# A linear-attention and Fourier-mixing kernel: the last additions and stores move into the other way of the closing branch, and the middle row's products get a stationary operand of 128 columns

## The chip, the cores and the metric

The kernel runs on one core of one Trainium2 chip. TensorE (PE) multiplies matrices, with the weight loads in a queue of their own (PEld); VectorE (DVE), ScalarE (ACT) and GpSimd (POOL) work element by element; SyncE (SP) issues transfers. A "q" behind an engine's name in a row of the profile stands for its sequencer: loads of registers, branches, waits and issues of transfers. The metric is the time of one execution on the device in microseconds (us), as the median of several runs; lower is better.

## The reference

The inputs are q, k, v and a gate, each of 4 batches, 8 heads, 768 steps and 48 channels, and two weight matrices of 384x1536 and 1536x384. All is float32 in the kernel.

```python
f = 1.0 / (1.0 + np.exp(-f_logit))
for t in range(S):
    state = f[:, :, t, :, None] * state + np.einsum('bhd,bhe->bhde', k[:, :, t], v[:, :, t])
    y[:, :, t] = np.einsum('bhd,bhde->bhe', q[:, :, t], state)
...
x = np.ascontiguousarray(attn_out.transpose(0, 2, 1, 3)).reshape(B, S, H * D)
...
X = np.fft.fft(x, axis=1)
X = np.fft.fft(X, axis=2)
mixed = np.real(X).astype(np.float32)
u = x + mixed
mu = np.mean(u, axis=-1, keepdims=True)
var = np.mean((u - mu) ** 2, axis=-1, keepdims=True)
un = (u - mu) / np.sqrt(var + 1e-06)
ch = np.maximum(un @ w_ch1, 0.0) @ w_ch2
return (u + ch).astype(np.float32)
```

## The kernel before

The kernel has four stages for each of the 4 batches, and works on several batches at once.

*Attention* works on 16 units (two heads of a batch each), in blocks of 128 steps: `attention`, `outputs`, `fold`. It leaves x, of 6 blocks of 128 tokens by 384 channels, and sums and differences of x for the Fourier stage in the tiles `ce`, `se`, `xc`, `xs`.

*The Fourier stage* is `fnet`: products with cosine and sine tables over the tokens (tile `z`, L740), over the channels (tile `mix`, L759, two blocks of tokens by symmetry), and for the middle row of the batch, a single token that belongs to no block, two products into the tile `mid` (L774). Their stationary operand is one column of `zz`, so they use one column of TensorE's array and write one row. In the program's terms a float32 product becomes two weight loads and two multiplications in the trace; the 8 products of the four batches are 16 rows. In batch 3 `mid` and `mix` stand in the middle of the previous batch's first layer (L861); in the others they stand behind products of the attention, of 48 rows and 64 columns.

*Normalisation* is `turn`: mean, deviation, and a turned copy of each block.

*The two layers* are `projected`, for a pair of blocks c and d at a time. The first layer (`hidden`, L861) forms 15 products by a scheme that saves some of 18, and the second one (L916) forms 7 products of 6 multiplications each where 8 would stand, from h and from sums of the second weight matrix made ahead. A pair's results are the halves c1, c2 of block c and d1, d2 of block d. They are gathered in two banks: tile `fx` has the halves X and Y, tile `fz` the halves V and Z. Product 6 goes on top of product 1 in X, product 7 on top of both; products 5 and 3 go into Z. The last pair of the last batch is (0, 4), and has an order of its own (L937 to L954): c1 is stored as soon as it is whole (L938), then come products 6, 5, 7 and 3. VectorE adds V to d1 (L940), X after product 6 to c2 (L943), Z after product 5 to d2 (L946), X after product 7 to d1 and d2 in one instruction (L949), which makes block d (token block 4) whole. SyncE stores it in three pieces (L714). Product 3 goes on top of product 5 in Z, and c2 gets Z with both in one addition (L952) and is stored last (L953).

*The order of all this* is written out by hand: the string `ORDER` holds 964 words, and each word takes one step of a stage (`P3` is one step of the last batch's `projected`). A step ends at a `yield`. Each engine runs its own instructions in that order.

*The general way.* The fast program is right for inputs within some bounds. The step `judge` (L984 to L994) works out a flag from what the kernel saw; it stands some 35 us ahead of the end. Behind the last step each engine loads the flag into a register (L1045) and branches on it (L1047). With the flag set, a general program of about 8000 instructions runs, which computes all again; with it not set, as with these inputs, the engines jump over it. In the code there is no other way, only the compiler's own: it waits until the engine's work is done, and sets the semaphores as the general program would have left them. Behind both stand the closing waits (L1131): SyncE waits for every transfer and every engine, and then the five engines meet twice.

SyncE's load of the flag is followed by two register instructions that check its bounds (FUSED_REGOPS and SEQ_ASSERT in the trace).

Of the kernel before, what the change touches and what calls it, by code (L numbers as in the profile page):

```python
# [7 lines left out]
F32 = mybir.dt.float32  # L8
U32 = mybir.dt.uint32
AF = mybir.ActivationFunctionType  # L10
ALU = mybir.AluOpType

C = 128
# [77 lines left out]
def kernel(  # L91
# [40 lines left out]
    y_out = ps_y.tile([128, 2, 512], F32, tag="y", name="y")  # L132
    spare = y_out[:, 0, 3 * C:]

    def fixed(shape, tag):
        return const.tile(shape, F32, tag=tag, name=tag)

# [3 lines left out]
    g_t = [fixed([128, S + 1], f"g{i}") for i in range(2)] + [wide_t[:, i * (S + 1):(i + 1) * (S + 1)] for i in range(2)]  # L141
    k_t = [fixed([128, S], f"k{i}") for i in range(2)] + [wide_t[:, 2 * S + 2:3 * S + 2]]
    q_t = [fixed([128, S], f"q{i}") for i in range(2)] + [wide_t[:, i * S + 2:(i + 1) * S + 2] for i in range(3, 5)]
    few = [True]

    def home(name, u):

        if few[0] and u >= 2 * HP:
# [569 lines left out]
    def fnet(b, x):  # L718
# [12 lines left out]
        rows_of = [hi - lo for _, lo, hi in terms]  # L731
        for T in (1, 3, 0, 2):
            src, lo, hi = terms[T]
            z = ps_f.tile([128, 512], F32, tag="f", name=f"z{b}_{T}")[:hi - lo]
            if T % 2 == 0:
                parts = [(slice(0, N), 3, 1), (slice(0, NQ, 2), 1, 0), (slice(1, NQ, 2), 0, 0), (OD, 2, 0)]
            else:
                parts = [(slice(0, N), 0, 1), (EV, 1, 0), (OD, 2, 0)]
            for i, (cols, j, t) in enumerate(parts):
                nc.tensor.matmul(z[:, cols], lhsT=src[:, j, lo:hi], rhs=tab[:, t, T % 2, cols],  # L740
                                 start=(i == 0), stop=(i == len(parts) - 1), skip_group_check=True)
            falls = down(z)[:, :QS // 2 - 1:-1]
            nc.scalar.copy(pairs(zz[:hi - lo, T, :QS]), up(z)[:, :QS // 2])
            nc.scalar.copy(pairs(zz[:hi - lo, T, 2 * C:3 * C]), falls[:, :C // 2])
            nc.scalar.copy(pairs(zz[:hi - lo, T, QS:2 * C]), falls[:, C // 2:])
            if T % 2 == 0:
                nc.scalar.copy(zz[:hi - lo, T, 3 * C:3 * C + 1], z[:, QS // 2:QS // 2 + 1])
            yield
# [2 lines left out]
        mv = p2.tile([128, NCH, 2], F32, tag="mv", name=f"mv{b}")  # L751
        rstd = p2.tile([128, NCH], F32, tag="rstd", name=f"rstd{b}")
        def mixed(c):
            mix = ps_f.tile([128, 512], F32, tag="f", name=f"mix{b}_{c}")
            for odd in range(2):
                o = slice(0, NQ) if not odd else slice(NQ, N)
                for i in range(2):
                    T = 2 * odd + i
                    nc.tensor.matmul(mix[:, o], lhsT=zz[:rows_of[T], T, PLACES[c]],  # L759
                                     rhs=cd[:rows_of[T], T, :NQ - odd], start=(i == 0), stop=(i == 1))  # L760
            return mix
# [3 lines left out]
        falling = lambda a, n: a[:, 1:2 * n - 1].rearrange("p (r m) -> p m r", r=2)[:, ::-1]  # L765


        mid = ps_f.tile([128, 512], F32, tag="f", name=f"mid{b}")
        row = p1.tile([128, DM], F32, tag="row", name=f"row{b}")
        by2 = lambda a: a.rearrange("p (m r) -> p m r", r=2)  # L770
        H1 = QD + 1
        for T, o in ((0, slice(0, H1)), (2, slice(H1, 2 * H1 - 1))):
            n = rows_of[T]
            nc.tensor.matmul(mid[0:1, o], lhsT=zz[:n, T, 3 * C:3 * C + 1], rhs=cd[:n, T, :o.stop - o.start],  # L774
                             start=True, stop=True)
        nc.vector.tensor_tensor(by2(row[0:1, :HD]), rising(mid[0:1], H1), by2(x[0:1, 3, :HD]), ALU.add)
        nc.vector.tensor_tensor(by2(row[0:1, HD:]), falling(mid[0:1], H1), by2(x[0:1, 3, HD:]), ALU.add)
# [12 lines left out]
        def turn(c):  # L790
            j, t = [(j, pair.index(c)) for j, pair in enumerate(pairs_of) if c in pair][0]
            if t == 0:
                turned[j] = p2.tile([128, 3, 2, 128], F32, tag="unT", name=f"unT{b}_{j}")
            un = p2.tile([128, DM], F32, tag="un", name=f"un{b}_{c}")
            nc.vector.tensor_scalar(un, x[:, c], mv[:, c, 0:1], rstd[:, c:c + 1], ALU.subtract, ALU.mult)
            yield
            pt = ps_f.tile([128, 512], F32, tag="f", name=f"pt{b}_{c}")
            for kt in range(3):
                nc.tensor.transpose(pt[:, kt * 128:(kt + 1) * 128], un[:, kt * 128:(kt + 1) * 128], ident)  # L799
            nc.scalar.copy(turned[j][:, :, t], pt[:, :DM].rearrange("p (k t) -> p k t", k=3))  # L800
# [42 lines left out]
    def hidden(name, unT, h):  # L843

        tokens = lambda i: unT[:, i % 3, i // 3 ^ FLIP] if i < 6 else sums[:, i - 6]
        opened = set()
        chains = {i: ps_a.tile([128, 512], F32, tag="sc", name=f"{name}_{i}") for i in range(2)}  # L850
        for made, a, w, chain, to, how, complete in PRODUCTS:
            for i, one, two, sign in made:
                add(tokens(i), tokens(one), tokens(two), sign)
            if made:
                yield
            new = chain not in opened
            opened.add(chain)
            if chain not in chains:
                chains[chain] = ps_f.tile([128, 512], F32, tag="f", name=f"{name}_{chain}")
            for m in range(4):  # L860
                nc.tensor.matmul(chains[chain][:, m * 128:(m + 1) * 128], lhsT=block(w)[:, m * 128:(m + 1) * 128],  # L861
                                 rhs=tokens(a), start=(new and m == 0), stop=True, skip_group_check=True)
            out = h[:, to % 3 * 4:to % 3 * 4 + 4, to // 3 ^ FLIP]
            got = chains[chain].rearrange("p (m n) -> p m n", n=128)
            first = how[0] == "="
            if first:
                kind = AF.Relu if complete else AF.Copy
                nc.scalar.activation(out, got, kind, scale=1.0 if how == "=+" else -1.0)  # L868
            else:
                nc.vector.tensor_tensor(out, out, got, ALU.add if how == "+" else ALU.subtract)  # L870
            if complete and not first:
                yield
                nc.scalar.activation(out, out, AF.Relu)  # L873
            yield

    def projected(b, x, again=False):
# [5 lines left out]
        for j, (c, d) in enumerate(PAIRS if b < B - 1 else LAST_PAIRS):  # L882
# [5 lines left out]
            if b and not again:  # L888
                yield from hidden(f"ub{b}_{j}", turned_of[b][j], h)
            for m in range(NF if again or not b else 0):  # L890
                pp = ps_f.tile([128, 512], F32, tag="f", name=f"up{b}_{j}_{m}")
                for kt in range(3):
                    nc.tensor.matmul(pp[:, :256], lhsT=w1[:, kt, m * 128:(m + 1) * 128], rhs=unT[:, kt],  # L893
                                     start=(kt == 0), stop=(kt == 2))
                nc.scalar.activation(h[:, m].rearrange("p t n -> p (t n)"), pp[:, :256], AF.Relu)  # L895
                yield
            if not again and (b, j) == (0, 0):

                for t, i in enumerate((c, d)):
                    po = ps_f.tile([128, 512], F32, tag="f", name=f"po{b}_{i}")  # L900
                    for m in range(NF):
                        nc.tensor.matmul(po[:, :DM], lhsT=h[:, m, t], rhs=w2[:, m],  # L902
                                         start=(m == 0), stop=(m == NF - 1))
                        if m in (2, 5, 8):
                            yield
                    tt(x[:, i], po[:, :DM], x[:, i], ALU.add)
                    store(b, i, x[:, i])
                    yield
                continue
# [6 lines left out]
                    nc.tensor.matmul(out, lhsT=h[:, m], rhs=blocks[i][:, m], start=(start and m == 0),  # L916
                                     stop=(m == H - 1), skip_group_check=True)

            fx = ps_f.tile([128, 512], F32, tag="f", name=f"fx{b}_{j}")
            X, Y = fx[:, :HD], fx[:, HD:2 * HD]  # L920
            product(1, X, h11, start=True)
            s1 = p1.tile([128, H, 128], F32, tag="s1", name=f"s1_{b}_{j}")
# [4 lines left out]
            tt(c1, X, c1, ALU.add)  # L927
            tt(h11, s1, h11, ALU.subtract)
            yield
            fz = ps_f.tile([128, 512], F32, tag="f", name=f"fz{b}_{j}")  # L930
            V, Z = fz[:, :HD], fz[:, HD:2 * HD]
            product(4, V, h22, start=True)
            tt(c1, Y, c1, ALU.add)
# [1 line left out]
            yield  # L935
            both = x[:, d].rearrange("p (a n) -> p a n", a=2)
            if (b, c) == (B - 1, 0):  # L937
                nc.sync.dma_start(out=out[b, :C, :HD], in_=c1)  # L938
                product(6, X, h11)
                tt(d1, V, d1, ALU.add)  # L940
                yield
                product(5, Z, s1)
                tt(c2, X, c2, ALU.add)  # L943
                yield
                product(7, X, h21)
                tt(d2, Z, d2, ALU.add)  # L946
                yield
                product(3, Z, h12)
                tt(both, X.unsqueeze(1).to_broadcast([128, 2, HD]), both, ALU.add)  # L949
                store(b, d, x[:, d])  # L950
                yield
                tt(c2, Z, c2, ALU.add)  # L952
                nc.sync.dma_start(out=out[b, :C, HD:], in_=c2)  # L953
                yield  # L954
                continue
            product(5, Z, s1)
# [13 lines left out]
            store(b, d, x[:, d])  # L970
            yield

    x_of, units, fronts, rest = {}, {}, {}, {}

    def x_all(b):
        if b not in x_of:
# [3 lines left out]
    def judge():  # L980
# [6 lines left out]
        nc.vector.tensor_scalar(most, most, SMALLEST, None, ALU.is_lt)  # L987
        nc.vector.scalar_tensor_tensor(most[:R], part[:R, 0:1], HIGH, most[:R], ALU.is_ge, ALU.max)
        nc.vector.scalar_tensor_tensor(most[:R], part[:R, 1:2], WARM, most[:R], ALU.is_ge, ALU.max)
        turned = ps_f.tile([128, 512], F32, tag="f", name="turned")  # L990
        nc.tensor.matmul(turned[0:1, :128], lhsT=most, rhs=ident, start=True, stop=True)
        nc.vector.tensor_reduce(most[0:1], turned[0:1, :128], mybir.AxisListType.X, ALU.max)
        flag = p1.tile([128, 1], mybir.dt.int32, tag="flag", name="flag")
# [50 lines left out]
    tc.no_sync_barrier()  # L1044
    again = nc.values_load(flag[0:1, 0:1], min_val=0, max_val=1)  # L1045
    few[0] = False
    with tc.If(again > 0):  # L1047
        if wide:
            for i, (dst, _, _) in enumerate(blocks_of):
                single_or_zero(dst, words(i))  # L1050
# [7 lines left out]
        for b in range(B):  # L1058
# [5 lines left out]
                pass  # L1064
            for _ in projected(b, x, again=True):
                pass


# [67 lines left out]
```

## Time and profile before

| what | value |
|---|---|
| median of 3 runs | 517.89 us (517.5 to 519.24) |
| the profiled execution | 521.55 us |
| its span, first to last instruction | 519.8 us |
| mean granted clock of TensorE | 0.98 |
| TensorE, multiplications | busy 488.9 us, 94% |
| TensorE, weight loads | busy 450.3 us, 87% |
| VectorE | busy 375.6 us, 72% |
| ScalarE | busy 217.6 us, 42% |
| GpSimd | busy 62.4 us, 12% |

The span lies within one profiled execution, which takes 1.75 us more than its span; the runs without a profile are shorter than the profiled one. Rows of the profile read "line engine operation out<-in". In a timeline the two first numbers are the start in us from the span's start and the length. In the rows of one line, three numbers with strokes between them are the shortest, median and longest duration in ns, and then come the first and the last start. L numbers are lines of the kernel before; the changed kernel's stand some 5 to 17 lower down.

### The profile page before, as it was taken

Reading aid. Unit: us, or ns where it says so; the run is one execution under the profiler, and the core shown is the slowest. Engines: PE = TensorE matmul, PEld = TensorE weight load, DVE = VectorE, ACT = ScalarE, POOL = GpSimd, SP = SyncE. Lnnn points to the kernel's source line nnn. Section 1 sums busy time; section 2 is a strip of 40 time slices with the busy share of each in tenths; the row PEclk is TensorE's granted clock in tenths of the full one; section 3 lists DMA queues with packets and bytes.
Section 4 is the critical chain, followed back from the end, with each engine's and each line's share of the span. In section 5 each row is a group of like instructions: output and inputs, shape, how many; then the busy total and the mean of one; then the engine's idle time right before and its main releaser. Section 6 shows DMA issues by size and latency. Waiting matters only on the chain.

```text
span 519.8 us, 13729 instructions
## 1 busy us (share of the span) xinstructions
PE 488.9 (94%) x5814; PEld 450.3 (87%) x5814; DVE 375.6 (72%) x746; ACT 217.6 (42%) x520; POOL 62.4 (12%) x85
## 2 busy tenths in 40 slices
PE   4588799989999999999999999999999999999994
PEld 4477678856898899999999899999999999999894
DVE  3868999864887478687687897689486658576561
ACT  6666469753442532462452445351431404032220
POOL 3114534541001000000001001000001000010100
PEclk9967999999999999999999999999999999999998
DMA  8987555585100420222210032101301214433001
GB/s 215 251 230 233 139 153 171 168 236 151 54 1 32 109 57 6 66 71 71 71 55 32 21 91 72 47 3 45 109 6 44 74 47 137 151 122 93 33 9 29
DMA packets 20649, 48.15 MB, mean 93 GB/s; under 512 B 3425, under 2 KB 6178, under 8 KB 20578
## 3 DMA queue, kind: packets, MB, share of 16 engines
q1 hardware_dynamic: 19474, 43.63, 29.7%
q0 software_dynamic: 1104, 3.54, 1.9%
q8 instruction: 48, 0.79, 0.7%
q14 instruction: 23, 0.19, 0.1%
HBM read 42.44 MB, written 4.72 MB: 91 GB/s over the span
## 4 chain that ended last, share of the span: by engine, by line
PE 82%; DMA 7%; DVE 3%; issue 2%; POOL 2%; ACT 2%; SPq 1%; DVEq 0%; POOLq 0%; ACTq 0%
PE ub L861 23%; PE fx L916 17%; PE fz L916 13%; PE up L893 8%; PE z L740 4%; DMA raw<-in_w_ch_dram 4%; PE mix L759 3%; PE y L568 3%; PE y L627 2%; PE po L902 2%; DMA k<-in_qkf_dram 2%; PE sc L409 2%; PE ds L610 2%; PE pt L799 1%; DMA tab<-in_seq_tab_dram 1%
## 5 line engine op out<-in xcount | busy, mean ns | idle before, releaser
L870 DVE TENSOR_TENSOR h<-h,ub 128x512 f32<-128x512 f32 x81 | 55.3, 685 | 36.7 <-PE ub L861 29.0
L708 POOL DMA_INDIRECT out_dram<-x,place x16 | 17.0, 1065 | 353.1 <-DVE x L966 227.6
L868 ACT ACTIVATE h<-ub 128x512 f32<-128x512 f32 x54 | 32.0, 593 | 46.8 <-PE ub L861 31.1
L893 PE MATMUL up<-unT,w 128*128 128x256 f32 x216 | 50.3, 383 | 0.0
L861 PE MATMUL ub<-wide,w 128*128 128x128 f32 x360 | 45.5, 276 | 2.4 <-DVE wide L833 2.4
L916 PE MATMUL fx<-block,h 128*128 128x192 f32 x264 | 46.6, 327 | 0.0
L861 PEld LDWEIGHTS ub<-wide,w 128*128 128x128 f32 x360 | 42.8, 192 | 3.4 <-PE pt L799 1.6
L916 PE MATMUL fx<-w,h 128*128 128x192 f32 x264 | 45.2, 327 | 0.0
L893 PEld LDWEIGHTS up<-unT,w 128*128 128x128 f32 x216 | 39.9, 190 | 5.7
L873 ACT ACTIVATE h<-h 128x512 f32<-128x512 f32 x45 | 28.4, 631 | 37.2 <-DVE h L870 37.2
L916 PEld LDWEIGHTS fx<-block,h 128*128 128x128 f32 x264 | 43.4, 190 | 0.1
L916 PEld LDWEIGHTS fx<-w,h 128*128 128x128 f32 x264 | 42.7, 190 | 0.2
L292 POOL TENSOR_TENSOR w<-w,raw 128x384 uint32<-128x384 uint32 x24 | 29.4, 1231 | 64.7 <-ACT raw L288 23.3
L861 PE MATMUL ub<-unT,w 128*128 128x128 f32 x288 | 36.9, 275 | 0.0
L861 PEld LDWEIGHTS ub<-unT,w 128*128 128x128 f32 x288 | 34.6, 192 | 0.0
L800 ACT COPY unT<-pt 128x384 f32<-128x384 f32 x24 | 11.3, 470 | 42.0 <-PE pt L799 41.7
L861 PE MATMUL ub<-unT,wide 128*128 128x128 f32 x216 | 28.7, 276 | 0.0
L861 PE MATMUL ub<-wide 128*128 128x128 f32 x216 | 28.5, 275 | 0.0
L386 DVE TENSOR_TENSOR_SCAN W<-g,bound 112x768 f32<-112x768 f32 x12 | 21.1, 1762 | 7.5 <-ACT g L380 7.5
L861 PEld LDWEIGHTS ub<-unT,wide 128*128 128x128 f32 x216 | 26.3, 192 | 0.2
L861 PEld LDWEIGHTS ub<-wide 128*128 128x128 f32 x216 | 26.3, 192 | 0.0
L895 ACT ACTIVATE h<-up 128x256 f32<-128x256 f32 x36 | 13.7, 382 | 25.9 <-PE up L893 25.9
(194 smaller groups left out, 996.8 us busy)
## 6 DMA issues: line engine op xcount, KB each, us to landing
raw<-in_w_ch_dram SPq DMA_DIRECT2D x24, 384.0 KB, 4.0
v<-in_v_dram SPq DMA_DIRECT2D x16, 288.0 KB, 4.8
k<-in_w_ch_dram SPq DMA_DIRECT2D x12, 384.0 KB, 3.8
g<-in_w_ch_dram SPq DMA_DIRECT2D x12, 384.0 KB, 3.2
k<-in_qkf_dram SPq DMA_DIRECT2D x14, 288.0 KB, 5.9
g<-in_qkf_dram SPq DMA_DIRECT2D x12, 288.0 KB, 5.4
q<-in_qkf_dram SPq DMA_DIRECT2D x12, 288.0 KB, 4.9
wide<-in_qkf_dram SPq DMA_DIRECT2D x10, 288.0 KB, 5.1
```

Of the source, the lines that this page charges most:

```text
L292: nc.gpsimd.tensor_tensor(bits, bits, lo, ALU.add)
L386: nc.vector.tensor_tensor_scan(W, g, bound[:R], 0.0, ALU.add, ALU.min)
L568: nc.tensor.matmul(y[FILL[g], c // 3, c % 3 * C + t.start:c % 3 * C + t.stop], lhsT=vals[rows, o:o + (64 if g == 0 else D)], rhs=weights, ...
L708: nc.gpsimd.indirect_dma_start(out=out.rearrange("b s d -> (b s) d"), out_offset=bass.IndirectOffsetOnAxis(ap=place[:, b, i:i + 1], axis=0 ...
L740: nc.tensor.matmul(z[:, cols], lhsT=src[:, j, lo:hi], rhs=tab[:, t, T % 2, cols], start=(i == 0), stop=(i == len(parts) - 1), skip_group_c ...
L759: nc.tensor.matmul(mix[:, o], lhsT=zz[:rows_of[T], T, PLACES[c]], rhs=cd[:rows_of[T], T, :NQ - odd], start=(i == 0), stop=(i == 1))
L861: nc.tensor.matmul(chains[chain][:, m * 128:(m + 1) * 128], lhsT=block(w)[:, m * 128:(m + 1) * 128], rhs=tokens(a), start=(new and m == 0) ...
L868: nc.scalar.activation(out, got, kind, scale=1.0 if how == "=+" else -1.0)
L870: nc.vector.tensor_tensor(out, out, got, ALU.add if how == "+" else ALU.subtract)
L873: nc.scalar.activation(out, out, AF.Relu)
L893: nc.tensor.matmul(pp[:, :256], lhsT=w1[:, kt, m * 128:(m + 1) * 128], rhs=unT[:, kt], start=(kt == 0), stop=(kt == 2))
L916: nc.tensor.matmul(out, lhsT=h[:, m], rhs=blocks[i][:, m], start=(start and m == 0), stop=(m == H - 1), skip_group_check=True)
```

## The change

There are three edits.

*The other way of the branch gets work.* The generator of the last pair stops behind product 3 until a list `closing` has an entry, which it gets when the branch is opened. The steps left are taken in an `Else` of the branch. They are four additions of VectorE and four stores of SyncE. The addition of Z to d2, which stood ahead of the branch, is among them. Product 3 no longer goes on top of product 5 in Z but into `last`, a piece of the bank `y_out`, which is the attention's. So c2 now gets Z (product 5) and `last` (product 3) in two additions. The results c2, d1 and d2 are gathered in the tile `xc` in place of x; ScalarE copies d2 there ahead of the branch.

*Other banks for the general way.* `bank` hands out the tiles that `fnet`, `turn`, `hidden`, `projected` and `judge` used to take from the pool `ps_f`: from that pool in the fast program, and from the attention's pool `ps_a` in the general one.

*The middle row.* The stationary operand of the two products, one column of `zz`, is read 128 times over, so that all 128 columns of the array hold the same numbers and all 128 rows of `mid` come out alike. The first row alone is used, as before.

```diff
+    def bank(name):
+        if few[0]:
+            return ps_f.tile([128, 512], F32, tag="f", name=name)
+        return ps_a.tile([128, 2, 512], F32, tag="sc", name=name)[:, 0]
...
-            nc.tensor.matmul(mid[0:1, o], lhsT=zz[:n, T, 3 * C:3 * C + 1], rhs=cd[:n, T, :o.stop - o.start],
+            nc.tensor.matmul(mid[:, o], lhsT=zz[:n, T, 3 * C:3 * C + 1].to_broadcast([n, 128]), rhs=cd[:n, T, :o.stop - o.start],
                              start=True, stop=True)
...
             if (b, c) == (B - 1, 0):
+                ends = xc.rearrange("p a n -> p (a n)")
+                c2_, d_ = ends[:, :HD], ends[:, HD:3 * HD]
+                last = y_out[:, 0, :HD]
                 nc.sync.dma_start(out=out[b, :C, :HD], in_=c1)
+                nc.scalar.copy(d_[:, HD:], d2)
                 product(6, X, h11)
-                tt(d1, V, d1, ALU.add)
+                tt(d_[:, :HD], V, d1, ALU.add)
                 yield
                 product(5, Z, s1)
-                tt(c2, X, c2, ALU.add)
+                tt(c2_, X, c2, ALU.add)
                 yield
                 product(7, X, h21)
-                tt(d2, Z, d2, ALU.add)
                 yield
-                product(3, Z, h12)
+                product(3, last, h12, start=True)
+                while not closing:
+                    yield
+                tt(d_[:, HD:], Z, d_[:, HD:], ALU.add)
+                tt(c2_, Z, c2_, ALU.add)
+                both = d_.rearrange("p (a n) -> p a n", a=2)
                 tt(both, X.unsqueeze(1).to_broadcast([128, 2, HD]), both, ALU.add)
-                store(b, d, x[:, d])
+                store(b, d, d_)
                 yield
-                tt(c2, Z, c2, ALU.add)
-                nc.sync.dma_start(out=out[b, :C, HD:], in_=c2)
+                tt(c2_, last, c2_, ALU.add)
+                nc.sync.dma_start(out=out[b, :C, HD:], in_=c2_)
                 yield
                 continue
...
-    with tc.If(again > 0):
+    with tc.If(again > 0) as both_ways:
+        closing.append(True)
...
+    with both_ways.Else():
+        for _ in rest[B - 1]:
+            pass
```

VectorE at the end of the last pair, before the change; x is the tile of the results, fx and fz the two banks, and the general way's instructions come behind the branch:

```order
L940 TENSOR_TENSOR x_3998<-fz_2_5185,x_3998 128x192
L943 TENSOR_TENSOR x_3998<-fx_2_5167,x_3998 128x192
L946 TENSOR_TENSOR x_3998<-fz_2_5185,x_3998 128x192
L949 TENSOR_TENSOR x_3998<-fx_2_5167,x_3998 128x384
L952 TENSOR_TENSOR x_3998<-fz_2_5185,x_3998 128x192
L1045 TENSOR_LOAD flag
L1047 COMPARE_AND_BRANCH
```

VectorE at the same place after the change; the rows left out are the general way, and the last four additions are the other way of the branch:

```order
L949 TENSOR_TENSOR xc<-fz_2_5185,x_3998 128x192
L952 TENSOR_TENSOR xc<-fx_2_5167,x_3998 128x192
L1058 TENSOR_LOAD flag
L1060 COMPARE_AND_BRANCH
...
L959 TENSOR_TENSOR xc<-fz_2_5185,xc 128x192
L960 TENSOR_TENSOR xc<-fz_2_5185,xc 128x192
L962 TENSOR_TENSOR xc<-fx_2_5167,xc 128x384
L965 TENSOR_TENSOR xc<-y,xc 128x192
```

The load of the flag and the branch have moved ahead of three additions, and a fourth addition, from the bank y, stands behind them.

SyncE at the end, before the change; the first row stores c1, the next three block d, the fifth c2:

```order
L938 DMA out_dram<-x_3998 128x192
L714 DMA out_dram<-x_3998 1x384
L714 DMA out_dram<-x_3998 15x384
L714 DMA out_dram<-x_3998 112x384
L953 DMA out_dram<-x_3998 128x192
L1045 TENSOR_LOAD flag
L1045 ISA x2
L1047 COMPARE_AND_BRANCH
```

SyncE at the same place after the change, again with the general way left out:

```order
L946 DMA out_dram<-x_3998 128x192
L1058 TENSOR_LOAD flag
L1060 COMPARE_AND_BRANCH
...
L719 DMA out_dram<-xc 1x384
L719 DMA out_dram<-xc 15x384
L719 DMA out_dram<-xc 112x384
L966 DMA out_dram<-xc 128x192
...
L1058 ISA x2
```

Four stores have moved behind the branch, and the two register instructions (the row with ISA) behind both ways.

More of the change, by code (lines that the diff above doesn't have):

```diff
@@ L133 @@
     spare = y_out[:, 0, 3 * C:]
+    def bank(name):
+        if few[0]:
+            return ps_f.tile([128, 512], F32, tag="f", name=name)
+        return ps_a.tile([128, 2, 512], F32, tag="sc", name=name)[:, 0]
+    few = [True]
     def fixed(shape, tag):
@@ L143 @@
     q_t = [fixed([128, S], f"q{i}") for i in range(2)] + [wide_t[:, i * S + 2:(i + 1) * S + 2] for i in range(3, 5)]
-    few = [True]
     def home(name, u):
@@ L733, in fnet @@
             src, lo, hi = terms[T]
-            z = ps_f.tile([128, 512], F32, tag="f", name=f"z{b}_{T}")[:hi - lo]
+            z = bank(f"z{b}_{T}")[:hi - lo]
             if T % 2 == 0:
@@ L753, in mixed @@
         def mixed(c):
-            mix = ps_f.tile([128, 512], F32, tag="f", name=f"mix{b}_{c}")
+            mix = bank(f"mix{b}_{c}")
             for odd in range(2):
@@ L765, in fnet @@
         falling = lambda a, n: a[:, 1:2 * n - 1].rearrange("p (r m) -> p m r", r=2)[:, ::-1]
-        mid = ps_f.tile([128, 512], F32, tag="f", name=f"mid{b}")
+        mid = bank(f"mid{b}")
         row = p1.tile([128, DM], F32, tag="row", name=f"row{b}")
@@ L796, in turn @@
             yield
-            pt = ps_f.tile([128, 512], F32, tag="f", name=f"pt{b}_{c}")
+            pt = bank(f"pt{b}_{c}")
             for kt in range(3):
@@ L858, in hidden @@
             if chain not in chains:
-                chains[chain] = ps_f.tile([128, 512], F32, tag="f", name=f"{name}_{chain}")
+                chains[chain] = bank(f"{name}_{chain}")
             for m in range(4):
@@ L890, in projected @@
             for m in range(NF if again or not b else 0):
-                pp = ps_f.tile([128, 512], F32, tag="f", name=f"up{b}_{j}_{m}")
+                pp = bank(f"up{b}_{j}_{m}")
                 for kt in range(3):
@@ L899, in projected @@
                 for t, i in enumerate((c, d)):
-                    po = ps_f.tile([128, 512], F32, tag="f", name=f"po{b}_{i}")
+                    po = bank(f"po{b}_{i}")
                     for m in range(NF):
@@ L917, in product @@
                                      stop=(m == H - 1), skip_group_check=True)
-            fx = ps_f.tile([128, 512], F32, tag="f", name=f"fx{b}_{j}")
+            fx = bank(f"fx{b}_{j}")
             X, Y = fx[:, :HD], fx[:, HD:2 * HD]
@@ L929, in projected @@
             yield
-            fz = ps_f.tile([128, 512], F32, tag="f", name=f"fz{b}_{j}")
+            fz = bank(f"fz{b}_{j}")
             V, Z = fz[:, :HD], fz[:, HD:2 * HD]
@@ L971, in projected @@
             yield
-    x_of, units, fronts, rest = {}, {}, {}, {}
+    x_of, units, fronts, rest, closing = {}, {}, {}, {}, []
     def x_all(b):
@@ L989, in judge @@
         nc.vector.scalar_tensor_tensor(most[:R], part[:R, 1:2], WARM, most[:R], ALU.is_ge, ALU.max)
-        turned = ps_f.tile([128, 512], F32, tag="f", name="turned")
+        turned = bank("turned")
         nc.tensor.matmul(turned[0:1, :128], lhsT=most, rhs=ident, start=True, stop=True)
```

## The prediction

> **What bounds the kernel now.** I read the page of the profile first, then the chain of waits over the last 40 us, then the timeline of the last 10 us, and last the single rows of the lines on which the closing branch stands, because the chain ends well before the span does. First the page:
>
> ```profile
> span 519.8 us, 13729 instructions
> ...
> PE 488.9 (94%) x5814; PEld 450.3 (87%) x5814; DVE 375.6 (72%) x746; ACT 217.6 (42%) x520; POOL 62.4 (12%) x85
> ...
> L861 PE MATMUL ub<-wide,w 128*128 128x128 f32 x360 | 45.5, 276 | 2.4 <-DVE wide L833 2.4
> ```
>
> TensorE is busy for 94% of the span, so nearly anywhere only an edit to its work can pay. The end is another matter. The chain of waits, its last pieces (start, length, what):
>
> ```profile
> 509.10 1.95 PE fx L916 x12
> 511.05 1.96 PE fz L916 x12
> ```
>
> TensorE's last product ends at 513.02 (511.05 + 1.96), and the span is 519.8. The timelines of the end (start, length) show VectorE's additions, SyncE's stores and ScalarE's last work:
>
> ```profile
> 507.19 0.36 DVE L943 TENSOR_TENSOR x<-fx,x 128x192 f32<-128x192 f32 x1 [1.28 <-PE fx L916]
> 509.14 0.36 DVE L946 TENSOR_TENSOR x<-fz,x 128x192 f32<-128x192 f32 x1 [1.59 <-PE fz L916]
> 511.09 0.56 DVE L949 TENSOR_TENSOR x<-fx,x 128x384 f32<-128x384 f32 x1 [1.59 <-PE fx L916]
> 513.04 0.36 DVE L952 TENSOR_TENSOR x<-fz,x 128x192 f32<-128x192 f32 x1 [1.39 <-PE fz L916]
> ```
>
> ```profile
> 504.84 0.34 SPq L938 DMA_DIRECT2D out_dram<-x  x1
> 511.72 1.46 SPq L714 DMA_DIRECT2D out_dram<-x  x3
> 513.42 0.35 SPq L953 DMA_DIRECT2D out_dram<-x  x1
> ```
>
> ```profile
> 499.60 0.58 ACT L868 ACTIVATE h<-ub 128x512 f32<-128x512 f32 x1
> ```
>
> VectorE's last addition ends at 513.40, so 6.4 us follow in which nothing is computed. What comes then is in the rows of the flag's load (L1045), of the branch (L1047) and of the closing lines (L1131); a row gives count, duration in ns, first and last start:
>
> ```profile
> L1045 DVEq TENSOR_LOAD <-flag x1: 541/541/541, 513.1 to 513.1; - x1
> L1045 SPq TENSOR_LOAD <-flag x1: 470/470/470, 513.8 to 513.8; - x1
> L1045 SPq FUSED_REGOPS  x1: 186/186/186, 514.4 to 514.4; - x1
> ```
>
> ```profile
> L1047 SPq EVENT_SEMAPHORE  x8: 17/17/17, 517.3 to 517.9; - x8
> ...
> L1047 ACTq COMPARE_BRANCH  x1: 50/50/50, 499.9 to 499.9; - x1
> L1047 ACTq EVENT_SEMAPHORE  x1: 17/17/17, 502.4 to 502.4; - x1
> L1047 PEldq COMPARE_BRANCH  x1: 3731/3731/3731, 510.5 to 510.5; - x1
> L1047 DVEq COMPARE_BRANCH  x1: 72/72/72, 513.7 to 513.7; - x1
> L1047 PEldq EVENT_SEMAPHORE  x1: 51/51/51, 514.3 to 514.3; - x1
> L1047 SPq COMPARE_BRANCH  x1: 50/50/50, 514.7 to 514.7; - x1
> L1047 DVEq EVENT_SEMAPHORE  x1: 21/21/21, 516.8 to 516.8; - x1
> ```
>
> ```profile
> L1131 SPq EVENT_SEMAPHORE  x14: 17/28/28, 517.9 to 519.8; - x14
> ...
> L1131 SPq DRAIN  x3: 7/13/116, 518.7 to 519.5; - x3
> ```
>
> The time from issue to landing of the last store, L953:
>
> ```profile
> DMA to landing us min/median/max: 1.8/1.8/1.8
> ```
>
> From an engine's branch to its first instruction behind it pass 2.4 us (ScalarE, 499.9 to 502.4), 2.6 (SyncE), 3.1 (VectorE) and 3.8 (TensorE), though the branch itself mostly takes 0.05 to 0.07. SyncE branches only after its last store, at 514.7, and is back at 517.3. That last store landed at 513.42 + 1.8 = 515.2, two us earlier. So the end is set by SyncE standing at its branch, with VectorE (back at 516.8) close behind; then come eight waits, the closing waits and the meetings of the engines, to 519.8. I take the standing time for the load of the code behind the branch. The Trainium skill, Runtime: NRT & Kernel Launch, section Instruction fetch mechanics, says that a taken branch to code outside the loaded pages must fetch it before going on; the rows agree, 2.4 to 3.8 us each.
>
> **The change part by part. The branch.** Behind product 6's addition (L943) VectorE now goes to the branch, and SyncE behind the store of L938. Four additions, four stores stand behind it. Each engine's stand at the branch so lies beside TensorE's products 7 and 3.
>
> VectorE: its load began with the last addition (513.04 and 513.1), the branch 0.6 later. So the branch stands at 507.2 + 0.6 = 507.8, and VectorE is back at 507.8 + 3.1 = 510.9. Until then it has nothing to miss: the product that L949 needs ends at 511.05. With 0.1 for a wait, the first addition starts at 511.0. L946's addition, moved here, and the new one that adds product 5 to c2 cost 0.36 each, as L946; L949's costs 0.56: end 511.0 + 0.36 + 0.36 + 0.56 = 512.3, where it ended at 511.65. The last addition waits for product 3 as before (513.04) and has 0.7 us of room.
>
> SyncE: it branches at 504.84 + 0.34 + 0.5 for the load, some 505.7, and is back by 508.3 (at its own 2.6) or 509.5 (at TensorE's 3.8), before VectorE's 512.3. Its three stores then start at 512.3 instead of 511.72, 0.6 later. The old last store waited for the last addition (513.40, issue 513.42); the new one waits for the three issues, 1.46 + 0.24 as before: 512.3 + 1.7 = 514.0. It lands at 514.0 + 1.8 = 515.8. SyncE itself issues until 514.35, has four waits left (eight took 0.6, so 0.3) and the two register instructions that now stand behind both ways (514.4 to 514.7, 0.3), and reaches the closing waits at 515.0. Twelve of the fourteen take 517.9 to 518.7, 0.067 each; the eighth is the last store's, reached 0.5 us after the first, 515.5, so it waits for the landing, 515.8. From the eighth wait to the end it took 519.8 - 518.4 = 1.4 (1.45 unrounded). New end 515.8 + 1.45 = 517.25: 2.55 us earlier. What is late next is no longer the branch but the landing of the last store, with the issue of three stores ahead of it.
>
> The bounds: with ScalarE's 2.4 VectorE is back at 510.2, and the additions wait for product 7 only, so stores start at 511.72 and the last at 513.42: end 516.65, gain 3.2. With TensorE's 3.8 everything is 0.7 later, gain 1.85. Inside the 1.46 one issue was slow:
>
> ```profile
> L714 SPq DMA_DIRECT2D out_dram<-x x15: 249/351/751, 120.3 to 512.4; - x15
> ```
>
> The longest issue took 0.75, the median is 0.35: three at the median give back 0.4, within these bounds.
>
> Edits with one answer: ScalarE's copy of 128x192 runs after its last work at 500.2, ten us before VectorE's use, at less than the 0.58 of that 128x512 row; its branch, 0.5 later, is hidden the same. If that cover went, it would cost its 0.58. Product 3 in a bank of its own saves TensorE nothing: the addition that it waited for ended at 509.50 and the product starts at 511.05. The scratch tile under the new results was last read by the batch's first products, which stand ahead of the middle row's at 376.45. The general way with its other banks does not run here.
>
> **The middle row.** The weight loads of the middle row and the products behind it, then the timeline of TensorE where the last of the four batches comes to it, and the first batch:
>
> ```profile
> L774 PEld LDWEIGHTS mid<-cd,zz x16: 79/83/86, 65.5 to 376.6; 97*1 97x1 f32 x8, 96*1 96x1 f32 x8
> ```
>
> ```profile
> L759 PE MATMUL mix<-cd,zz x96: 323/326/431, 65.9 to 383.4; 96*128 96x192 f32 x48, 97*128 97x193 f32 x24, 95*128 95x193 f32 x24
> ```
>
> ```profile
> 375.80 0.72 PE L861 MATMUL ub<-wide,w 128*128 128x128 f32 x5
> 376.45 0.49 PE L774 MATMUL mid<-cd,zz 97*1 97x97 f32 x4
> 376.88 1.41 PE L759 MATMUL mix<-cd,zz 97*128 97x193 f32 x7
> ```
>
> ```profile
> 65.01 0.55 PE L585 MATMUL sc<-q,g 48*64 48x64 f32 x24
> 65.49 0.49 PE L774 MATMUL mid<-cd,zz 97*1 97x97 f32 x4
> 65.91 1.09 PE L759 MATMUL mix<-cd,zz 97*128 97x193 f32 x5
> ```
>
> A 128-column stream runs at (0.72 - 0.28) / 4 = 0.11 us an instruction, five in 0.72 with 0.28 for the last. Its fifth starts at 376.25, the one-column products not at 376.36 but at 376.45, and the first product after them takes 0.43 where 0.33 is the median: going to one column and back costs 0.1 each time. Four mids at 0.11 in the stream end at 376.36 + 0.44 = 376.80, against 376.88 + 0.1 = 376.98: 0.18 us saved. In the first batch the stream ahead is of 64 columns, so one break stays: 65.49 + 0.1 + 0.44 = 66.03 against 65.91 + 0.1 = 66.01, nothing. With two further batches like the first, -0.1 in sum. The ends: -0.7 (0.18 in all four) and +0.5 (sixteen instructions 0.03 longer, 0.08 to 0.11). That a single column is read 128 times over, no row shows. The Trainium skill, TensorEngine Tiling (Array Packing), Key Properties, says that changing the tiling mode drains the array. By that rule each batch loses one break of about 0.1 and the last two, and the sum would be -0.5.
>
> Sum: -2.55 - 0.1 = -2.65 us. The profiled execution took 521.55 for its 519.8 span, 3.7 above the median of the runs, 517.89; I take the change off both: 518.9 there, span 517.15, and 515.2 for the median.
>
> **The rivals.** *A second stand.* Code of the new way that lies in two pieces stops VectorE or SyncE once more. For it: the way now holds waits, additions and stores. Against it: SyncE runs all its closing waits, 517.3 to 519.8, with no stop. VectorE back at 510.9 + 2.6 = 513.5 ends the third addition at 514.9; everything is 2.6 later, the gain is gone: 517.8. SyncE alone, stopped after its last store, has the landing as cover for 0.8 of it: its closing waits start at 515.0 + 2.6 = 517.6 and take 1.9 to the end, 519.5: gain 0.3 + 0.1, 517.5.
>
> *It does not do so much outside the profile.* The runs are 3.7 us shorter than the profiled execution; if loads of code are a part of that, SyncE's 2.6 may be 1.4 there, and the gain 1.35 + 0.1: 516.4. Against it: that difference can lie anywhere in the 520 us.
>
> *Slower: the stand moves in front of the stores.* The Trainium skill's section on instruction fetch speaks against running work behind a taken branch. In this kernel: if VectorE stands twice at the longest row, 3.8, it is back at 507.8 + 7.6 = 515.4, ends the third addition at 516.8, and the stores start at 516.8 instead of 511.72. That is 4.5 later than forecast: 4.5 - 2.65 = 1.85 slower, 519.7. It decides from a stand of 507.8 to 513.5 on, 5.7 us, nearly twice VectorE's row.
>
> **How the numbers follow.** About 0.3%, 1.55 us, is what a measurement of this kernel can tell from no change. Forecast, 515.2: chance 0.68. Its own range is 517.89 - 3.2 - 0.7 = 514.0 to 517.89 - 1.85 + 0.5 = 516.5. Second stand 0.15, less outside the profile 0.10, slower 0.07. Faster by over 0.3% (under 516.3): 0.68. Within: the two middle rivals, less than 0.01 of them beyond, 0.24. Slower: 0.08. The range 514.0 to 517.6 takes in the forecast, the third case and the half of the second, and leaves out less than 2 in 10.
>
> **What would show it.** VectorE's and SyncE's branches near 507.8 and 505.7, their first instructions behind it near 510.9 and 508.4; the last addition at 513.0 as now; the last store issued at 513.4 to 514.0; closing waits that end on its landing; a span of some 517.2. Mids at 0.11 us in the stream. It is wrong if either engine's first instruction behind the branch comes after 513, if a second gap stands behind it, or if TensorE's last product moves by more than 0.7 us.

## The result, and the profile after

The changed kernel took 514.83 us in the median of 22 runs, the kernel before 517.91 in the median of 22 beside them. The ratio is 0.9938, with a 95% interval from 0.9921 to 0.9954: 3.2 us less, between 2.4 and 4.1. The forecast was 2.65 us less. Here and below, where a ratio is given, the difference in us is worked out from it, and the ratio is not exactly that of the two medians (3.1 us here).

The profiled execution took 513.87 us, for a span of 512.1. Its page, the same rows as before:

```profile
span 512.1 us, 13731 instructions
...
PE 490.7 (96%) x5814; PEld 453.2 (88%) x5814; DVE 377.4 (74%) x747; ACT 217.5 (42%) x521; POOL 60.4 (12%) x85
```

The last pieces of its chain of waits:

```profile
500.79 1.95 PE fx L921 x12
502.74 1.95 PE fz L921 x12
504.69 1.95 PE fx L921 x12
506.64 1.96 PE y L921 x12
```

These are products 6, 5, 7 and 3. TensorE's last product ends at 508.60, and 3.5 us follow to the end of the span. Before they were 6.8 (513.02 to 519.8). I call this stretch the tail and read each kernel's from its own last product, since one execution differs from the next by more than the change. VectorE and SyncE at the end:

```profile
502.77 0.36 DVE L952 TENSOR_TENSOR xc<-fx,x 128x192 f32<-128x192 f32 x1 [1.28 <-PE fx L921]
506.40 0.36 DVE L959 TENSOR_TENSOR xc<-fz,xc 128x192 f32<-128x192 f32 x1 [3.27 <-issue]
506.67 0.35 DVE L960 TENSOR_TENSOR xc<-fz,xc 128x192 f32<-128x192 f32 x1
506.94 0.55 DVE L962 TENSOR_TENSOR xc<-fx,xc 128x384 f32<-128x384 f32 x1
508.62 0.36 DVE L965 TENSOR_TENSOR xc<-y,xc 128x192 f32<-128x192 f32 x1 [1.14 <-PE y L921]
```

```profile
500.43 0.34 SPq L946 DMA_DIRECT2D out_dram<-x  x1
507.51 1.41 SPq L719 DMA_DIRECT2D out_dram<-xc  x3
509.10 0.36 SPq L966 DMA_DIRECT2D out_dram<-xc  x1
```

The branches and the first instructions behind them are in the rows of three lines, the branch (L1060), the first addition behind it (L959) and the closing waits (L1148), whose semaphores SyncE now meets first:

```profile
L1060 SPq COMPARE_BRANCH  x1: 50/50/50, 501.4 to 501.4; - x1
L1060 DVEq COMPARE_BRANCH  x1: 72/72/72, 503.4 to 503.4; - x1
L1060 PEldq COMPARE_BRANCH  x1: 3881/3881/3881, 506.1 to 506.1; - x1
L1060 PEldq EVENT_SEMAPHORE  x1: 51/51/51, 510.1 to 510.1; - x1
```

```profile
L959 DVEq EVENT_SEMAPHORE  x1: 49/49/49, 506.3 to 506.3; - x1
```

```profile
L1148 SPq EVENT_SEMAPHORE  x18: 17/28/28, 504.0 to 512.1; - x18
```

The stands are all still there: VectorE's from 503.4 to 506.3, SyncE's from 501.4 to 504.0, 2.9 and 2.6 us. VectorE's gap is the 3.27 in the row of L959, put down to "issue", time in which it waited for nothing that the profile shows. But SyncE's lies beside products 6 and 5 and VectorE's beside 5 and 7, and both are over before product 3 begins at 506.64. TensorE's own stand, from 506.1 to 510.1, outlasts its last product, but not the landing of the last store, which ends at 510.9 (below). The last store goes out 0.50 us behind TensorE's last product, where it was 0.40 before, and now SyncE is past its branch at that time.

The middle row's place in the last batch, the timeline of TensorE:

```profile
371.44 0.83 PE L866 MATMUL ub<-wide,w 128*128 128x128 f32 x6
372.12 0.58 PE L779 MATMUL mid<-cd,zz 97*128 97x97 f32 x4
372.54 1.34 PE L764 MATMUL mix<-cd,zz 97*128 97x193 f32 x7
```

From the start of the last ub product (371.44 + 5 x 0.11 = 372.0) to the first mix product there are 0.54 us, where there were 0.63 (376.25 to 376.88), and the first mix product takes 0.36 where it took 0.43.

### The profile page after: what moved, and what is told of

It reads as the page before. It is cut to its first block, busy times and chain, and to the rows that moved or that the text cites. A ratio compares the mean times of both kernels' runs of the same rounds, so it can differ in the third digit from the quotient of the medians.

```text
span 512.1 us, 13731 instructions
## 1 busy us (share of the span) xinstructions
PE 490.7 (96%) x5814; PEld 453.2 (88%) x5814; DVE 377.4 (74%) x747; ACT 217.5 (42%) x521; POOL 60.4 (12%) x85
## 4 chain that ended last, share of the span: by engine, by line
PE 77%; DVE 4%; DMA 1%; issue 1%; POOL 0%; ACT 0%; POOLq 0%; ACTq 0%
PE ub L866 24%; PE fx L921 17%; PE fz L921 12%; PE up L898 6%; PE z L745 3%; PE mix L764 2%; PE y L573 2%; PE po L907 2%; DMA raw<-in_w_ch_dram 1%; PE y L632 1%; PE sc L414 1%; PE ds L615 1%; PE pt L804 1%; PE yt L653 1%; DVE w L296 1%; DVE w L295 1%
```

## The experiments

The theory is that of the prediction: code behind the branch has to be loaded, each engine stands there while it is, and the change pays because the stand now lies beside TensorE's last products. I tested three rivals: that the middle row made the gain; that work behind the branch pays by itself, through fewer closing waits; that the stand is the price of any branch and no load of code.

**The branch alone.** The changed kernel with the middle row as it was:

```diff
-            nc.tensor.matmul(mid[:, o], lhsT=zz[:n, T, 3 * C:3 * C + 1].to_broadcast([n, 128]), rhs=cd
+            nc.tensor.matmul(mid[0:1, o], lhsT=zz[:n, T, 3 * C:3 * C + 1], rhs=cd
```

> The changed kernel with the middle row's products back at one column. Theory (the engines stand at the branch beside TensorE's last two products): all of the gain but 0.1 us stays, 3.1 us below the kernel before, and from the end of TensorE's last product to the end of the span 3.5 us, as in the changed kernel (6.8 before). Rival (the gain is made by the middle row, since TensorE's last product ended 4.4 us earlier in the changed kernel's trace): the time is that of the kernel before within 1 us.

Measured: ratio 0.9934 to the kernel before (0.9909 to 0.9959), medians 515.18 and 518.37 us: 3.4 us less, between 2.1 and 4.7. Its last product and its span:

```profile
506.38 1.96 PE y L921 x12
```

```profile
core 0: 511.7 us, clock 0.990
```

The last product ends at 508.34, so the tail is 3.4 us. The branch alone has all of the gain that can be measured.

**The middle row alone.** The kernel before with the opposite edit:

```diff
-            nc.tensor.matmul(mid[0:1, o], lhsT=zz[:n, T, 3 * C:3 * C + 1], rhs=cd
+            nc.tensor.matmul(mid[:, o], lhsT=zz[:n, T, 3 * C:3 * C + 1].to_broadcast([n, 128]), rhs=cd
```

> The kernel before with the middle row's products on 128 columns and nothing else. Theory: 0.1 us below the kernel before, nothing that the time can show; from the last product behind the middle row's to the second product after them 0.72 us in the last batch (0.90 before) and 0.86 in the other three (0.84 before); 6.8 us from TensorE's last product to the end. Rival (the gain is made here): 3 us below the kernel before.

Measured: ratio 1.0001 (0.9973 to 1.0029), at most 1.4 us less. Its last product ended at 509.01 of a span of 516.0, a tail of 7.0. In its trace, from the last product ahead of the middle row's to the second behind them, the last batch took 0.72 us and the others 0.86, as expected and as in the changed kernel. This rival falls. The run also shows what not to read from one execution: its last product ended 4 us earlier than in the profiled execution of the kernel before, with no shorter tail and 0.1 us of change ahead of it.

**A late branch.** The changed kernel, with three of the four additions and three of the four stores taken ahead of the branch:

```diff
                 product(3, last, h12, start=True)
-                while not closing:
-                    yield
                 tt(d_[:, HD:], Z, d_[:, HD:], ALU.add)
                 tt(c2_, Z, c2_, ALU.add)
                 both = d_.rearrange("p (a n) -> p a n", a=2)
                 tt(both, X.unsqueeze(1).to_broadcast([128, 2, HD]), both, ALU.add)
                 store(b, d, d_)
                 yield
+                while not closing:
+                    yield
                 tt(c2_, last, c2_, ALU.add)
```

> The changed kernel with only the last addition and the last store behind the branch; the other three additions and three stores stand ahead of it. Theory (what pays is that the stand at the branch lies beside TensorE's products): SyncE branches only after its three stores, 1.0 to 1.1 us behind TensorE's last product, stands for 2.6, issues the last store at 3.8, which lands at 5.6; the span ends 6.7 to 7.1 us behind the last product, so the time is that of the kernel before within 0.5 us. Rival (work behind the branch pays by itself, through fewer closing waits or shorter meetings of the engines): at least 1.5 us below the kernel before.

Measured: ratio 0.9975 (0.9945 to 1.0005), 1.3 us less, between 2.9 less and 0.3 more. The chain of waits, behind product 7; product 3 follows it and ends 1.96 later, at 510.5:

```profile
506.60 1.96 PE fx L921 x12
508.57 0.02 issue
508.59 0.56 DVE xc L960
509.14 0.08 issue
509.22 0.07 DVEq L1060
509.29 3.01 issue
512.30 0.05 DVEq L965
512.36 0.04 issue
512.40 0.36 DVE xc L965
```

```profile
509.18 1.47 SPq L719 DMA_DIRECT2D out_dram<-xc  x3
514.23 0.37 SPq L966 DMA_DIRECT2D out_dram<-xc  x1
```

VectorE's stand of 3.0 us is now a piece of the chain itself, and its last addition comes at 512.40, 1.9 us after TensorE has finished. SyncE's branch, and its first semaphore behind it:

```profile
L1060 SPq COMPARE_BRANCH  x1: 50/50/50, 511.6 to 511.6; - x1
```

```profile
L1148 SPq EVENT_SEMAPHORE  x15: 17/28/28, 514.1 to 517.1; - x15
```

The last addition had ended at 512.76, and the last store still went out at 514.23, when SyncE was back, 3.7 us behind the product instead of 0.5. So it is SyncE's stand that ends this span; the run moves both engines' branches and does not show what VectorE's alone would cost. The span was 517.2, a tail of 6.7, against 6.8 to 7.0 with no work behind the branch and 3.5 in the changed kernel. There is work behind the branch here, too, and it earns next to nothing: the place of the branch decides. The tails show this; the time alone does not, since its interval holds both the theory's 0.5 us and the rival's 1.5.

**No general program, kernel before.** The way for the flag set holds one load, so that the closing code lies close behind the branch. This leaves out the general computation:

```diff
     with tc.If(again > 0):
-        if wide:
...
+        nc.sync.dma_start(out=causal.rearrange("p (i n) -> p i n", n=32), in_=sel)
```

> The kernel before without its general program: the way taken with the flag set holds one small load instead of some 8000 instructions, so the code behind the branch lies close by. It leaves out the general computation, which these inputs don't need. Theory (the stand at the branch is the load of far-off code): SyncE and VectorE stand under 0.6 us instead of 2.6 and 3.1; the landing of the last store, 2.2 us behind TensorE's last product, and sixteen waits behind it then set the end, 4.3 to 4.7 us behind the last product instead of 6.8, and the time is 2.1 to 2.5 us below the kernel before. Rival (a branch on a loaded register has this price wherever its target lies): stands of 2.4 to 3.8 us as before, and the time of the kernel before.

Measured: ratio 0.9957 (0.9937 to 0.9977), 2.2 us less, between 1.2 and 3.3. The rows of the branch:

```profile
L1047 PEldq COMPARE_BRANCH  x1: 236/236/236, 507.8 to 507.8; - x1
L1047 DVEq COMPARE_BRANCH  x1: 72/72/72, 511.0 to 511.0; - x1
L1047 SPq COMPARE_BRANCH  x1: 50/50/50, 511.6 to 511.6; - x1
L1047 SPq EVENT_SEMAPHORE  x1: 17/17/17, 511.8 to 511.8; - x1
```

The branch has the same work ahead of it and the same flag, and SyncE stands 0.2 us instead of 2.6. TensorE's branch took 0.24 us instead of 3.7. So no fixed price of a branch is left to speak of. That the stand is a load, the packets show that the profile counts as instructions; a row gives queue, number of packets, MB and share. From ScalarE's branch to the end, 499.9 to 519.8, the kernel before has

```profile
q8 instruction: 3, 0.05, 1.1%
q14 instruction: 6, 0.05, 0.9%
```

and this run, over the same stretch, 497.1 to 513.9, has

```profile
q8 instruction: 1, 0.02, 0.5%
```

On q14 nothing moves, and the one packet on q8 comes at 505.9, ahead of the branches of TensorE, VectorE and SyncE (507.8, 511.0 and 511.6). The tail was 3.6 us (510.25 to 513.9), less than the 4.3 to 4.7 that I expected: with little in the general program, SyncE has one wait in place of eight on the way taken, about 0.5 us, and a stop of some 0.3 us in its closing waits is gone, too (see below).

**No general program, changed kernel.** The same edit on the changed kernel.

> The changed kernel without its general program, the same way as the run before it. It leaves out the general computation, which these inputs don't need. Theory (the stands are hidden in the changed kernel): though they shrink from 2.6 and 2.9 us to under 0.6, the span ends 3.2 to 3.5 us behind TensorE's last product, as in the changed kernel (3.5), and the time is 3.0 to 3.6 us below the kernel before. Rival (part of the stand is still paid in the changed kernel): over 0.5 us below the changed kernel's 3.5 us.

Measured: ratio 0.9928 (0.9893 to 0.9962), 3.7 us less than the kernel before, between 2.0 and 5.5, where 3.0 to 3.6 were expected. Its tail was 3.3 us, last product 508.14, span 511.4, and its last stores:

```profile
506.80 1.11 SPq L719 DMA_DIRECT2D out_dram<-xc  x3
508.55 0.36 SPq L966 DMA_DIRECT2D out_dram<-xc  x1
```

The stores of block d start 1.34 us ahead of the last product's end here, 1.09 in the changed kernel, and yet the tails differ by 0.2 us. So the change hides all but 0.2 us, at most, of what far-off code costs this kernel; the measured times cannot tell this run from the changed kernel.

**Forty-eight more products of the middle row's kind,** one ahead of each product of the mixing step, once of one column on the kernel before, and once of 128 on the kernel with the wide middle row:

```diff
+                    if few[0]:
+                        nc.tensor.matmul(spare[0:1, :QD + 1], lhsT=zz[:QD + 1, 0, 3 * C:3 * C + 1], rhs=cd[:QD + 1, 0, :QD + 1],
+                                         start=True, stop=True, skip_group_check=True)
```

The wide form writes `spare[:, :QD + 1]` and reads the column 128 times over. The piece of the bank is not unused, as the expectation calls it: both forms change the attention's sums and so the result; the order and number of all other work stay.

> The kernel before with 48 more products of the middle row's kind, one column wide, into an unused piece of a bank, one ahead of each of the 48 products of the mixing step; nothing reads them. Each is two pairs of instructions. Theory (a change between one column and 128 costs about 0.1 us each way on top of the instructions): each takes 2 x 0.08 + 0.2 to 0.3 us, some 0.4 us, 48 of them 17 to 22 us on top of the kernel before. Rival (a change costs nothing between full products, what was seen is the load of the weights alone): 2 x 0.08 to 2 x 0.11 us each, 8 to 11 us.

> The same 48 products on 128 columns, and the middle row's own as in the changed kernel, on the kernel before; nothing reads the 48. Theory: each takes 2 x 0.11 us in the stream, 48 of them 10 to 12 us on top of the kernel before, 7 to 11 us less than the one-column form. Rival: no less than the one-column form, 0 to 2 us more.

Measured, one run each beside a median of 517.97 for the kernel before: 538.53 with one column, 530.84 with 128, so 20.6 and 12.9 us more, the second just above the 10 to 12 expected; the runs of the kernel before lie between 516.3 and 522.7. The timelines of TensorE, first one column, then 128 (y is the bank that the extra products write):

```profile
193.31 0.33 PE L760 MATMUL y<-cd,zz 97*1 97x97 f32 x2
193.57 0.59 PE L762 MATMUL mix<-cd,zz 95*128 95x193 f32 x2
194.09 0.33 PE L760 MATMUL y<-cd,zz 97*1 97x97 f32 x2
194.35 0.59 PE L762 MATMUL mix<-cd,zz 96*128 96x192 f32 x2
194.87 0.33 PE L760 MATMUL y<-cd,zz 97*1 97x97 f32 x2
```

```profile
192.94 0.36 PE L760 MATMUL y<-cd,zz 97*128 97x97 f32 x2
193.13 0.52 PE L762 MATMUL mix<-cd,zz 96*128 96x192 f32 x2
193.49 2.60 PE L919 MATMUL fx<-w,h 128*128 128x192 f32 x15
```

An extra and a mixing product, two instructions each, repeat every 0.78 us with one column (193.31, 194.09, 194.87) and take 0.55 with 128 (192.94 to 193.49). A mixing product alone takes 0.33. So the narrow product costs 0.45 us though it streams for only 2 x 0.08, and the wide one 0.22, just its stream. Forty-eight of them make 21.6 and 10.6 us, near the 20.6 and 12.9 of the single runs. The change of form costs 0.45 - 0.16, nearly 0.3 us, there and back. By the starts it is not the same each way: the mixing product's second instruction is followed by the narrow one 0.09 us late, and coming back takes 0.20 (0.09 ahead of the mixing product, 0.10 within it). The prediction's 0.1 for the way back, read off the duration of the first product behind the narrow ones, leaves out the 0.09 ahead of it. Where in TensorE this time goes, no run shows. The rival price for the narrow one, 8 to 11 us in all, is out.

## Why the prediction was right, point by point

**What bounds the end: right, and shown.** The prediction took the stand at the branch for a load of code and SyncE's for the one that ends the span. The short general program shows the first, the late branch shows what a stand costs when nothing covers it. Counted from the end of TensorE's last product, VectorE and SyncE branched 5.2 and 7.2 us ahead of it and were back 2.3 and 4.6 ahead; the forecast had 5.2 and 7.3, 2.1 and 4.6. One reading in it was wrong, with no effect on the sum: the stands do not lie beside products 7 and 3. By the prediction's own figures (505.7 to 508.3 and 507.8 to 510.9) they lie beside 6, 5 and 7, as the traces have them.

**VectorE behind the branch: right, 0.4 us too careful.** Forecast was a branch 0.6 us behind L943's start, a stand of 3.1 and the three additions in 1.28 us one after the other. Measured: 0.6, then 2.9, and the additions start 0.27 apart (506.40, 506.67, 506.94), since the next starts before the last has ended. They end 1.1 us ahead of TensorE's last product, not 0.7.

**SyncE's stores: the mechanism right, 0.5 us too late.** The last store went out 0.50 us behind TensorE's last product; forecast was 0.98. Of this, 0.4 is VectorE's, the rest the issues of the three stores, which go out within 1.41 instead of 1.46 and leave less to wait.

**The end behind the last store: the term that was mis-sized.** The row of the last store (L966):

```profile
DMA to landing us min/median/max: 1.8/1.8/1.8
```

Issued at 509.10, it was in at 510.9, and this is what SyncE waits for, as said. From there to the end I put 1.45 us, taken from the closing waits of the kernel before; it was 512.1 - 510.9 = 1.2. A little of this is my reading of the old row, which gives 1.41, not 1.45. The rest lies in that row itself: SyncE's last meeting there had a stop. The two profiles' rows of it:

```profile
L1131 SPq DRAIN  x3: 7/13/116, 518.7 to 519.5; - x3
```

```profile
L1148 SPq DRAIN  x3: 7/7/13, 511.3 to 511.6; - x3
```

The first and last of the three stood 0.8 us apart, and the longest took 116 ns; now they stand 0.3 apart. The prediction said that SyncE ran its closing waits with no stop, and that was wrong by some 0.3 us. The stop is there in the kernel before and with the middle row alone, and gone in the changed kernel, with the late branch and with the near code. One more load of code fits: in the kernel before one packet of instructions moves on q14 from 517.4 to 518.9, just ahead of the stop, and in the changed kernel none moves there behind 508. Which engine the packet is for, the trace does not say. In sum the tail lost 3.3 us where 2.55 were forecast, 0.5 by the earlier store and 0.25 by this.

**The middle row: right to the hundredth, in part by luck.** Forecast 0.18 us saved in the last batch and 0.02 lost in each other; the traces have 0.90 to 0.72 and 0.84 to 0.86. But of the 0.18, 0.08 were to come ahead of the first mix product and 0.10 within it, and it was 0.10 and 0.07. The other sum named there, -0.5, did not come: it was -0.1 over the four batches. The interval of the run with this edit alone contains no change.

**The rivals.** No second stand came behind the branch. That the gain is smaller outside the profile is out: the runs show 3.2 us, the tails 3.3. The Trainium skill, Runtime: NRT & Kernel Launch, section Instruction fetch mechanics, says that a taken branch to code that is not loaded has to wait for it, and names this as one reason why runtime control flow is expensive. The late branch agrees: VectorE's stand of 3.0 us ended 1.8 us behind TensorE's last product, and SyncE's 3.5 behind it. It does not count against this change, where the engines had that time to spare.

**One sign of the prediction misled.** It called itself wrong if TensorE's last product moved by more than 0.7 us, and in the two profiled executions it moved by 4.4. But the profiled execution of the kernel before was longer than all 22 runs beside the changed kernel, 521.55 against a median of 517.91 and at most 520.84, and the middle row of the first batch already stood 3.1 us earlier in the changed kernel's trace (62.4 against 65.5), ahead of anything that the change touches. With the medians less their tails and the 1.75 us outside the span, 517.91 - 6.8 - 1.75 = 509.4 and 514.83 - 3.5 - 1.75 = 509.6, the work ahead of the tail takes the same time, if the tails of the runs are those of the profiles.

## What to carry to other kernels

Where a kernel ends in a branch over a long program, look at each engine's first instruction behind it: here an engine stood 2.4 to 4.0 us for code that lay far off and 0.2 to 0.3 for code that lay close. Take the branch as early as the flag allows and give the way that is taken the last dependent work, so that the stand lies beside another engine's work; VectorE's branch 4 us later, with SyncE's behind its stores, gave the gain away again here. And compare the ends of two traces from their last product on, not by their spans, when executions differ by more than the change.

## What the runs showed of the hardware that was not expected

TensorE's branch itself lasts as long as its stand, 3.4 to 3.9 us in its row, and 0.24 with near code, while the other engines' branches take 0.05 to 0.07 and the stand shows as an empty gap behind them. A product of a single column among full ones costs twice what the same product costs on all 128 columns, 0.45 us against 0.22.
